# Sliding-window attention beside a Fourier mixing layer: transposed outputs written into the bytes of their chunk's sums, the halves in a tile of their own, and VectorE's sum of value products queued behind its latest low half

## The chip, the cores and the metric

The kernel runs on one core of a Trainium2 chip. The metric is the device time of one execution in microseconds (us). Three timed runs of the kernel before gave 1701.39, 1704.11 and 1705.67 us; the median is 1704.11 us. All engines named here belong to the one core: TensorE (PE in the profile; PEld is its weight load), VectorE (DVE), ScalarE (ACT), GpSimd (POOL) and SyncE (SP), which here issues nearly all DMAs.

## The reference

Two independent layers on a sequence of 2048 rows and 1024 columns; their outputs stand side by side. The first is attention with 32 heads of 32 columns, in which a query sees the 256 keys up to its own. The second multiplies by two Fourier matrices along the columns and two along the rows and keeps the real part.

```python
qkv = (x @ wqkv).reshape(B, S, 3, H, Dh)           # H = 32, Dh = 32
scores = einsum("bhqd,bhkd->bhqk", q, k) * Dh ** -0.5
mask = (i - j >= 0) & (i - j < 256)
o = einsum("bhqk,bhkd->bhqd", softmax(where(mask, scores, -1e9)), v)
a = o.reshape(B, S, D) @ wo

p = einsum("bsd,ed->bse", x, dft_hid_re); r = einsum("bsd,ed->bse", x, dft_hid_im)
b = einsum("ts,bse->bte", dft_seq_re, p) - einsum("ts,bse->bte", dft_seq_im, r)
out = concatenate([a, b], axis=-1)
```

## The kernel before

Every float32 operand is split into a high and a low half in float16, and a product is made of three float16 products (high by high, high by low, low by high). The big products are made first for the queries, keys and values, then for the Fourier layer in 48 units, then for the output projection. The units and the projection use a scheme of seven products for eight (the function `seven`, whose bank names a, b, c give the matmul names p_a, p_b, p_c).

Attention is not a stage of its own. It is a generator (`attention`) that the big products pull forward a step at a time (`tick`), from the value projection on to the last quarter of the Fourier layer. TensorE therefore runs one fixed stream in which attention's small matmuls stand between big ones: all matmuls that go through `mm` are held in program order.

Attention works on 256 blocks, each of 128 queries for two heads. Four blocks make a chunk; there are 64 chunks, and the names end in group, head pair and chunk, so that o_6_1_0 is chunk 52 counted from 0. For a block b:

- `s_step(b)`: TensorE writes the scores s (three PSUM banks in turn) and those of the farthest key block, far. VectorE masks them with a predicated copy (L259) and takes the maximum mx (L261). ScalarE makes the bias (L264), two exponentials (L271) and the high half hl (L274). VectorE makes the low half (L275). SP transposes both halves into t (L277).
- `z_step(b)`, two to four blocks later: GpSimd masks the transposed probabilities into z and t (L289, L291).
- `v_step(b)`, six blocks later and for two blocks at once (a pair; pair p is blocks 2p and 2p + 1, and its bank is named pv_2p): TensorE writes the value products, for the high and the low value columns, into the one PSUM bank with the tag "pv". VectorE adds the two (L323, a TENSOR_REDUCE) into the chunk's tile o. This sum frees the bank. The scale transposes of the Fourier units (pt_u) use the same bank.
- `o_step`, after a chunk's second sum: VectorE takes the reciprocal of the softmax sums (L332), GpSimd multiplies (L334), ScalarE and GpSimd split the product into the halves tile ohl (L337, L338), and SP transposes it into the tile ot (L340). The store of ot to the DRAM tensor ots (L360) waits in a list; it is issued in the step in which a fourth block of a chunk is started, behind the newest transpose.

The tiles o, ohl and ot of all chunks share one tag with three buffers: each new tile takes one that has been given back.

Each engine takes its instructions strictly in the order of its own queue. Where nothing in the code fixes the order, the compiler's scheduler sets it. `tc.issue_after(x)` tells the scheduler to place an instruction behind x in the queue; it adds no wait of its own. The list `behind` holds VectorE's latest low half: that of a block (L275), of a projection's output (L962, or L122 through `vec`), or the add that ends a Fourier product (L1045).

Of the kernel before, what the change touches and what calls it, by code (L numbers as in the profile page):

```python
# [9 lines left out]
F32 = mybir.dt.float32  # L10
F32R = mybir.dt.float32r
F16 = mybir.dt.float16
# [4 lines left out]
ALU = mybir.AluOpType  # L17
AX = mybir.AxisListType

P = 128  # L20
# [3 lines left out]
DH = 32  # L24
# [6 lines left out]
QB = CH // P  # L31
# [22 lines left out]
def fused_kernel(ctx: ExitStack, tc: tile.TileContext, xa, wqk, wv, wo, xb, wd, cs, out):  # L54
    nc = tc.nc
# [57 lines left out]
    def mm(*args, **kwargs):  # L113
        with tc.issue_after(fixed[0].ins) if fixed else nullcontext():
            fixed[:] = [nc.tensor.matmul(*args, **kwargs)]  # L115
        return fixed[0]
# [22 lines left out]
    behind = []  # L139
# [71 lines left out]
    def attention():  # L211
        att = cell["att"]
# [3 lines left out]
        st, cur, q2s, k2s, vts, store_o = {}, {}, {}, {}, {}, []  # L216
# [78 lines left out]
        def v_step(b):  # L295

            g, hp, sc, i = blocks[b]
            pvb = ps_v.tile([P, CH], F32, tag="pv", name=f"pv_{b}")
            pvt = pvb[:, :4 * VW].rearrange("p (r h w) -> p r h w", r=2, h=2)
            if (g, hp, sc) not in cur:  # L300
                cur[g, hp, sc] = att.tile([P, QB, 2, DH + 1], F32, tag="o", bufs=3, name=f"o_{g}_{hp}_{sc}")
            for r in (1, 0):
                qb = sc * QB + i + r
                nb = min(qb + 1, 3)
                nt = min(nb, 2)
                d = st[b + r]

                def weights(part, j, kb):
                    if nb == 3 and kb == 0:
                        return d["z"][:, part * 2 + j]  # L310
                    return d["t"][:, (part * 2 + j) * nt + kb - (nb - nt)]

                seq = [(0, kb) for kb in range(nb)] + [(1, kb) for kb in range(nb)]
                for j in range(2):
                    at = j * VW
                    for m, (part, kb) in enumerate(seq):
                        w = VW if part == 0 else DH + 1
                        k = qb + 1 - nb + kb
                        mm(pvt[:, r, j, :w], weights(part, j, kb),
                           vts[g, hp, k // QB][:, k % QB, at:at + w],  # L320
                                         start=(m == 0), stop=(m == len(seq) - 1),
                                         skip_group_check=True)
            nc.vector.tensor_reduce(cur[g, hp, sc][:, i:i + 2], pvt.rearrange("p r h (k w) -> p r h w k", k=2),  # L323
                                    axis=AX.X, op=ALU.add)
            del st[b], st[b + 1]

        def o_step(g, hp, sc):

            o = cur.pop((g, hp, sc))
            rs = att.tile([P, 2 * QB], F32, tag="rs", name=f"rs_{g}_{hp}_{sc}")  # L330
            on = o.rearrange("p i h w -> p (i h) w")
            nc.vector.reciprocal(rs, on[:, :, DH])  # L332
            on = on[:, :, :DH]
            nc.gpsimd.tensor_tensor(on, on, rs.unsqueeze(2).to_broadcast([P, 2 * QB, DH]), op=ALU.mult)  # L334
            o = o[:, :, :, :DH]
            ohl = att.tile([P, QB, 2, DH, 2], F16, tag="o", bufs=3, name=f"ohl_{g}_{hp}_{sc}")
            nc.scalar.activation(ohl[:, :, :, :, 0], o, AF.Copy)  # L337
            nc.gpsimd.tensor_tensor(ohl[:, :, :, :, 1], o, ohl[:, :, :, :, 0], op=ALU.subtract)  # L338
            ot = att.tile([P, QB, P], F16, tag="o", bufs=3, name=f"ot_{g}_{hp}_{sc}")
            nc.sync.dma_start_transpose(ot, ohl.rearrange("p i h d a -> p (i h d a)"))  # L340
            store_o.append((ots[sc, g, hp].rearrange("c a t -> (c a) t"), ot.rearrange("p i q -> p (i q)")))

        for b in range(nblk + LAG):
            for j in range(2):
                yield (blocks[b][0], blocks[b][2]) if b < nblk else None
                if b < nblk and j == 0:
                    s_step(b, 0)
                    s_step(b, 1)
                if j == 1 and b % 2 == 0 and b >= LAG:
                    v_step(b - LAG)  # L350
                    g, hp, sc, i = blocks[b - LAG + 1]
                    if i == QB - 1:
                        o_step(g, hp, sc)
                if j == 1 and b % 2 == ZAT and 3 <= b < nblk + 4:
                    for m in (b - 3 - (ZAT == 0), b - 2 - (ZAT == 0)):
                        if 0 <= m < nblk:
                            z_step(m)
                if j == 1 and store_o and (b >= nblk or blocks[b][3] == 3):
                    with tc.issue_after(line[0].ins):
                        nc.sync.dma_start(*store_o.pop(0))  # L360
                if j == 1 and b < nblk and blocks[b][3] == 1 and b + 3 < nblk:
                    g, hp, sc, _ = blocks[b + 3]
                    if (g, sc) in ready:
                        do_load(g, hp, sc)
                if j == 1 and b < nblk and blocks[b][3] == 3 and b + 1 < nblk:
                    g, hp, sc, _ = blocks[b + 1]
                    if (g, sc) in ready:
                        do_load_v(g, hp, sc)
# [526 lines left out]
    with tc.tile_pool(name="pa", bufs=3) as pa:  # L895
# [43 lines left out]
        for n, (kd, g, c) in enumerate(order):  # L939
# [12 lines left out]
            if kd == "v":  # L952
# [6 lines left out]
                f = vf[:, g, t // 4:t // 4 + 1]  # L959
# [137 lines left out]
    with tc.tile_pool(name="pb", bufs=1) as pb:  # L1097
# [45 lines left out]
        for n, (kind, p, c, i) in enumerate(units):  # L1143
# [35 lines left out]
            f = fu.pop(n)  # L1179
# [75 lines left out]
```

## Time and profile before

| what | before |
|---|---|
| median of 3 runs | 1704.11 us (1701.39 to 1705.67) |
| the profiled execution | 1701.5 us, of which the span is 1699.8 us |
| TensorE busy | 1688.6 us (99%) |
| VectorE busy | 1299.0 us (76%) |
| ScalarE busy | 1168.5 us (69%) |
| GpSimd busy | 575.2 us (34%) |
| sums of value products (L323) | 128, 425 ns each |
| stores of transposed outputs (L360) | 64, 128 KB each |

The profile is one execution. A row of the timeline gives the start and the length in us, the engine, the line, the operation, the tiles out<-in, and in square brackets how long the engine sat idle before it and what ended that. Buffer numbers are left out of the names there. A row of the waits gives who waited for whom, the total in us, how often, and the longest. Rows of one engine can overlap by about 0.1 us.

### The profile page before, as it was taken

The numbers are of one execution on the slowest core, as the hardware profiler recorded it, in microseconds if no ns is written. First come the engines' busy times: TensorE is split into PE (matmuls) and PEld (weight loads), VectorE is DVE, ScalarE is ACT, GpSimd is POOL, SyncE is SP. The second block draws the span as 40 slices with busy tenths as digits, with TensorE's granted clock in tenths as the row PEclk, the third lists the DMA queues.
The fourth block names the chain that finished last, engine by engine and source line by source line (L and its number), as shares of the span: only waits on it lengthen the run. The fifth ranks groups of instructions, "written<-read, shape, count | busy, mean of one in ns | idle before, by whom it ended". The sixth has DMA issues, their size and how long they took to land.

```text
span 1699.8 us, 30887 instructions
## 1 busy us (share of the span) xinstructions
PE 1688.6 (99%) x11007; PEld 847.7 (50%) x11007; DVE 1299.0 (76%) x2223; ACT 1168.5 (69%) x2035; POOL 575.2 (34%) x874
## 2 busy tenths in 40 slices
PE   9999999999999999999999999999999999999999
PEld 4444544555555555555554555545545545444444
DVE  7657787888987789897688896688876698687442
ACT  4476666676876787887787886688877688563322
POOL 0001222344434441444423565434555425411000
PEclk9999999999999999999999999999999999999999
DMA  6677999999999985987997999986989976866431
GB/s 244 240 267 245 252 289 269 282 264 306 256 240 209 211 220 127 206 194 184 232 251 236 199 186 176 227 197 127 190 161 204 226 183 137 177 180 121 115 99 75
DMA packets 469899, 348.63 MB, mean 205 GB/s; under 512 B 376944, under 2 KB 409968, under 8 KB 468848
## 3 DMA queue, kind: packets, MB, share of 16 engines
q1 hardware_dynamic: 462064, 321.48, 75.7%
q0 software_dynamic: 7680, 25.17, 9.5%
q8 instruction: 86, 1.41, 0.4%
q14 instruction: 69, 0.57, 0.1%
HBM read 166.99 MB, written 106.17 MB: 161 GB/s over the span
## 4 chain that ended last, share of the span: by engine, by line
PE 90%; DVE 3%; DMA 3%; ACT 2%; issue 1%; SPq 0%; POOL 0%; DVEq 0%; ACTq 0%; POOLq 0%
PE p_a L115 25%; PE pv L115 13%; PE p_b L115 12%; PE pq L115 10%; PE pk L115 10%; PE p_c L115 6%; PE po_a L115 5%; PE s L115 3%; PE po_b L115 2%; PE far L115 1%; PE po_c L115 1%; DMA ots<-ot 1%; DMA raw_wo<-in_wo_dram 1%; DVE reg L850 0%; DMA t<-hl 0%
## 5 line engine op out<-in xcount | busy, mean ns | idle before, releaser
L271 ACT ACTIVATE s<-s,bias,escs 128x256 f32<-128x256 f32 (+1 forms) x512 | 270.0, 528 | 11.7
L289 POOL TENSOR_SCALAR_AFFINE_SELECT z<-t 128x512 f16<-128x512 f16 x224 | 183.8, 828 | 162.2 <-PE pv L115 140.3
L264 ACT ACTIVATE bias<-mx,pshift,escs 128x2 f32<-128x2 f32 x256 | 98.4, 384 | 172.0 <-DVE mx L261 171.3
L275 DVE TENSOR_TENSOR hl<-s,hl 128x512 f16<-128x512 f32 (+1 forms) x256 | 170.2, 665 | 51.6 <-ACT hl L274 50.8
L115 PEld LDWEIGHTS <-reg 128*128 128x128 f16 x1344 | 128.9, 98 | 141.5
L291 POOL TENSOR_SCALAR_AFFINE_SELECT t<-t 128x512 f16<-128x512 f16 x224 | 187.8, 847 | 11.3
L115 PE MATMUL p_a<-reg,un_c 128*128 128x512 f16 x768 | 181.4, 379 | 0.6 <-DVE reg L850 0.3
L115 PE MATMUL pk<-reg,wu_k 128*128 128x512 f16 x768 | 174.2, 379 | 0.0
L268 POOL TENSOR_SCALAR mark<-bias 128x1 f32<-128x1 f32 x128 | 52.5, 410 | 358.3 <-ACT bias L264 333.6
L261 DVE TENSOR_REDUCE mx<-s 128x2 f32<-128x512 f32 (+1 forms) x256 | 170.9, 668 | 3.5
L115 PE MATMUL pv<-reg,reg 128*128 128x512 f16 x768 | 172.5, 379 | 0.0
L115 PEld LDWEIGHTS <-un_c 128*128 128x128 f16 x1152 | 109.9, 97 | 121.5 <-issue 2.2
L115 PEld LDWEIGHTS <-un_b 128*128 128x128 f16 x1152 | 109.6, 97 | 117.7 <-issue 0.9
L115 PEld LDWEIGHTS <-un_a 128*128 128x128 f16 x1152 | 109.4, 97 | 116.5
L115 PE MATMUL pq<-reg,wu_q 128*128 128x512 f16 x696 | 156.3, 379 | 0.0
L274 ACT ACTIVATE hl<-s 128x512 f16<-128x512 f32 (+1 forms) x256 | 148.8, 581 | 6.9 <-DMA t<-hl 1.4
L115 PE MATMUL p_a<-reg,un_b 128*128 128x512 f16 x576 | 136.4, 379 | 0.3 <-DVE y L1045 0.2
L115 PE MATMUL p_c<-reg,un_a 128*128 128x512 f16 x576 | 136.5, 379 | 0.0
L115 PE MATMUL p_b<-reg,un_b 128*128 128x512 f16 x576 | 136.3, 379 | 0.1
L115 PE MATMUL p_a<-reg,un_a 128*128 128x512 f16 x576 | 136.1, 379 | 0.0
L259 DVE COPY_PREDICATED s<-upper,far 128x256 f32<-128x256 uint32 x224 | 94.3, 421 | 46.3 <-PE s L115 45.3
L115 PEld LDWEIGHTS <-qk 96*128 96x128 f16 x1056 | 87.7, 97 | 66.4 <-issue 4.9
(216 smaller groups left out, 3139.7 us busy)
## 6 DMA issues: line engine op xcount, KB each, us to landing
raw_u<-in_cs_dram SPq DMA_DIRECT2D x64, 512.0 KB, 5.0
qk<-qk SPq DMA_DIRECT2D x64, 384.0 KB, 4.7
out_dram<-y POOLq DMA_DIRECT2D x72, 256.0 KB, 6.3
raw_wd<-in_wd_dram SPq DMA_DIRECT2D x24, 512.0 KB, 5.6
vs<-yv SPq DMA_DIRECT2D x32, 264.0 KB, 4.5
vt<-vs SPq DMA_DIRECT2D x64, 132.0 KB, 4.7
qk<-yq SPq DMA_DIRECT2D x32, 256.0 KB, 4.5
raw_wo<-in_wo_dram SPq DMA_DIRECT2D x16, 512.0 KB, 8.4
```

The source lines that it names most:

```text
L115: fixed[:] = [nc.tensor.matmul(*args, **kwargs)]
L259: nc.vector.copy_predicated(s[:, :, P:], upper2, d["far"] if nb == 3 else never2)
L261: nc.vector.tensor_reduce(mx, sv, axis=AX.X, op=ALU.max, negate=True)
L264: nc.scalar.activation(bias, mx, AF.Identity, bias=pshift, scale=es)
L268: marks[:] = [nc.gpsimd.tensor_scalar(mark, bias[:, 0:1], 1.0, None, op0=ALU.mult)]
L271: nc.scalar.activation(sv[:, h], sv[:, h], AF.Exp, bias=bias[:, h:h + 1], scale=es)
L274: nc.scalar.activation(hi, sv, AF.Copy)
L275: behind[:] = [nc.vector.tensor_tensor(lo, sv, hi, op=ALU.subtract)]
L289: nc.gpsimd.affine_select(out=z, in_=pk, compare_op=ALU.is_gt, fill=0.0, base=0, pattern=[[0, 4], [-1, P]], channel_multiplier=1)
L291: nc.gpsimd.affine_select(out=pk, in_=pk, compare_op=ALU.is_ge, fill=0.0, base=0, pattern=[[0, 4], [1, P]], channel_multiplier=-1)
```

## The change

Three things are edited.

- The chunk's tile o gets the tag to itself, with two buffers. The halves tile ohl gets a tag of its own with one buffer.
- The transposed output ot is no longer a tile. It is written, as float16, over the first 1024 of the 1056 bytes per partition of its own chunk's tile o, whose sums have been read by then. The store reads from there.
- The sum of value products is placed with `tc.issue_after(behind[0].ins)`, behind VectorE's latest low half.

Instructions, their shapes and the bytes moved stay the same. In the changed file the lines after the first edit stand one to three lower: the sum is L325, the reciprocal L335, the transpose L343, the store L363.

```diff
             if (g, hp, sc) not in cur:
-                cur[g, hp, sc] = att.tile([P, QB, 2, DH + 1], F32, tag="o", bufs=3, name=f"o_{g}_{hp}_{sc}")
+                cur[g, hp, sc] = att.tile([P, QB * 2 * (DH + 1)], F32, tag="o", bufs=2, name=f"o_{g}_{hp}_{sc}")
...
-            nc.vector.tensor_reduce(cur[g, hp, sc][:, i:i + 2], pvt.rearrange("p r h (k w) -> p r h w k", k=2),
-                                    axis=AX.X, op=ALU.add)
+            o = cur[g, hp, sc].rearrange("p (i h w) -> p i h w", i=QB, h=2)
+            with tc.issue_after(behind[0].ins):
+                nc.vector.tensor_reduce(o[:, i:i + 2], pvt.rearrange("p r h (k w) -> p r h w k", k=2),
+                                        axis=AX.X, op=ALU.add)
             del st[b], st[b + 1]
 
         def o_step(g, hp, sc):
 
-            o = cur.pop((g, hp, sc))
+            held_o = cur.pop((g, hp, sc))
+            o = held_o.rearrange("p (i h w) -> p i h w", i=QB, h=2)
...
-            ohl = att.tile([P, QB, 2, DH, 2], F16, tag="o", bufs=3, name=f"ohl_{g}_{hp}_{sc}")
+            ohl = att.tile([P, QB, 2, DH, 2], F16, tag="ohl", bufs=1, name=f"ohl_{g}_{hp}_{sc}")
...
-            ot = att.tile([P, QB, P], F16, tag="o", bufs=3, name=f"ot_{g}_{hp}_{sc}")
+            ot = held_o.bitcast(F16)[:, :QB * P].rearrange("p (i q) -> p i q", i=QB)
             nc.sync.dma_start_transpose(ot, ohl.rearrange("p i h d a -> p (i h d a)"))
             store_o.append((ots[sc, g, hp].rearrange("c a t -> (c a) t"), ot.rearrange("p i q -> p (i q)")))
```

TensorE's order is the same but for the scale transposes pt, of which some stand a few matmuls later. VectorE's order changes as follows at three places. In the rows, a name ends in the tile's number; a bracket names the semaphores that the instruction waits for, where DMAHW is a DMA queue and _49 only marks the build.

The first place is chunk 52's first sum (pair 104, blocks 208 and 209), in VectorE's queue of the kernel before.

```order
L261 TENSOR_REDUCE mx_214_15657<-s_214_15651 128x2 [waits DVE_49]
L122 SCALAR_TENSOR_TENSOR un33_a_15677<-raw_u33_0_15324,sc_u33_15635,un33_a_15677 128x1024 [waits DMAHW5_49,Activation_49]
L323 TENSOR_REDUCE o_6_1_0_15688<-pv_208_15687 128x132 [waits DMAHW3_49,DMAHW2_49,DMAHW6_49,DMAHW0_49,PE_49]
L807 TENSOR_TENSOR raw_u33_0_15324<-raw_u33_0_15324,raw_u33_1_15129 128x512 [waits DVE_49]
L275 TENSOR_TENSOR hl_213_15612<-s_213_15598,hl_213_15612 128x512 [waits DMAHW5_49,Activation_49]
L807 TENSOR_TENSOR raw_u33_1_15129<-raw_u33_1_15129 128x512 [waits DVE_49]
L259 COPY_PREDICATED s_215_15716<-upper_90,far_1040 128x2x128 [waits PE_49]
L261 TENSOR_REDUCE mx_215_15722<-s_215_15716 128x2 [waits DVE_49]
L122 SCALAR_TENSOR_TENSOR reg1_83<-raw_u33_1_15129,sc_u33_15635,reg1_83 128x512 [waits Activation_49]
L275 TENSOR_TENSOR hl_214_15663<-s_214_15651,hl_214_15663 128x512 [waits DMAHW2_49,Activation_49]
```

The same place in the changed kernel.

```order
L275 TENSOR_TENSOR hl_213_15560<-s_213_15546,hl_213_15560 128x512 [waits DMAHW5_49,Activation_49]
L122 SCALAR_TENSOR_TENSOR un33_a_15625<-raw_u33_0_15273,sc_u33_15583,un33_a_15625 128x1024 [waits DMAHW7_49,Activation_49]
L259 COPY_PREDICATED s_215_15664<-upper_90,far_1040 128x2x128 [waits PE_49]
L810 TENSOR_TENSOR raw_u33_0_15273<-raw_u33_0_15273,raw_u33_1_15079 128x512 [waits DVE_49]
L122 SCALAR_TENSOR_TENSOR reg1_83<-raw_u33_1_15079,sc_u33_15583,reg1_83 128x512 [waits Activation_49]
L261 TENSOR_REDUCE mx_215_15670<-s_215_15664 128x2 [waits DVE_49]
L275 TENSOR_TENSOR hl_214_15611<-s_214_15599,hl_214_15611 128x512 [waits DMAHW7_49,Activation_49]
L325 TENSOR_REDUCE o_6_1_0_15636<-pv_208_15635 128x132 [waits DMAHW4_49,DMAHW0_49,Pool_49]
L810 TENSOR_TENSOR raw_u33_1_15079<-raw_u33_1_15079 128x512 [waits DVE_49]
L259 COPY_PREDICATED s_216_15717<-upper_90,far_1040 128x2x128 [waits PE_49]
```

The sum stood ahead of the low halves of blocks 213 and 214 and of the masking of s_215; now it stands behind all three. It waits for DMA queues in both. Of the 64 first sums of a chunk, 10 wait for a DMA queue in the kernel before and 62 in the changed one.

The second place is chunk 54's second sum (pair 109, blocks 218 and 219), in VectorE's queue of the kernel before.

```order
L261 TENSOR_REDUCE mx_224_16285<-s_224_16281 128x2
L122 RECIPROCAL sc_u35_16254<-sc_u35_16254 128x1
L787 TENSOR_SCALAR fu35_16260<-fa_108,sc_u35_16254 128x1
L323 TENSOR_REDUCE o_6_1_2_16189<-pv_218_16309 128x132
L332 RECIPROCAL rs_6_1_2_16335<-o_6_1_2_16189 128x8
L122 SCALAR_TENSOR_TENSOR un35_a_16297<-raw_u35_0_15891,sc_u35_16254,un35_a_16297 128x1024
L259 COPY_PREDICATED s_225_16362<-upper_90,never_93 128x2x128
L807 TENSOR_TENSOR raw_u35_0_15891<-raw_u35_0_15891,raw_u35_1_15740 128x512
L122 SCALAR_TENSOR_TENSOR reg1_83<-raw_u35_1_15740,sc_u35_16254,reg1_83 128x512
L261 TENSOR_REDUCE mx_225_16366<-s_225_16362 128x2
L807 TENSOR_TENSOR raw_u35_1_15740<-raw_u35_1_15740 128x512
L275 TENSOR_TENSOR hl_224_16291<-s_224_16281,hl_224_16291 128x256
```

The same place in the changed kernel.

```order
L275 TENSOR_TENSOR hl_223_16190<-s_223_16176,hl_223_16190 128x512
L790 TENSOR_SCALAR fu35_16206<-fa_108,sc_u35_16200 128x1
L122 SCALAR_TENSOR_TENSOR un35_a_16243<-raw_u35_0_15838,sc_u35_16200,un35_a_16243 128x1024
L810 TENSOR_TENSOR raw_u35_0_15838<-raw_u35_0_15838,raw_u35_1_15688 128x512
L259 COPY_PREDICATED s_225_16307<-upper_90,never_93 128x2x128
L122 SCALAR_TENSOR_TENSOR reg1_83<-raw_u35_1_15688,sc_u35_16200,reg1_83 128x512
L810 TENSOR_TENSOR raw_u35_1_15688<-raw_u35_1_15688 128x512
L275 TENSOR_TENSOR hl_224_16237<-s_224_16227,hl_224_16237 128x256
L325 TENSOR_REDUCE o_6_1_2_16135<-pv_218_16255 128x132
L261 TENSOR_REDUCE mx_225_16311<-s_225_16307 128x2
L810 TENSOR_TENSOR raw_u35_1_15688<-raw_u35_1_15688,raw_u35_0_15838 128x512
L335 RECIPROCAL rs_6_1_2_16281<-o_6_1_2_16135 128x8
```

The sum moved behind the low half of block 224 and the five instructions in front of that; the reciprocal moved with it.

The third place is chunk 63's first sum (pair 126, blocks 252 and 253), near attention's end, in VectorE's queue of the kernel before.

```order
L122 RECIPROCAL sc_u44_18585<-sc_u44_18585 128x1 [waits DVE_49]
L787 TENSOR_SCALAR fu44_18591<-fa_108,sc_u44_18585 128x1
L122 SCALAR_TENSOR_TENSOR un44_a_18643<-raw_u44_0_18309,sc_u44_18585,un44_a_18643 128x1024 [waits DMAHW2_49,Activation_49]
L323 TENSOR_REDUCE o_7_1_3_18610<-pv_252_18609 128x132 [waits PE_49,Pool_49]
L807 TENSOR_TENSOR raw_u44_0_18309<-raw_u44_0_18309,raw_u44_1_18127 128x512 [waits DMAHW3_49,DVE_49]
L807 TENSOR_TENSOR raw_u44_1_18127<-raw_u44_1_18127 128x512 [waits DVE_49]
```

The same place in the changed kernel.

```order
L122 RECIPROCAL sc_u44_18522<-sc_u44_18522 128x1 [waits DVE_49]
L790 TENSOR_SCALAR fu44_18528<-fa_108,sc_u44_18522 128x1
L325 TENSOR_REDUCE o_7_1_3_18547<-pv_252_18546 128x132 [waits DMAHW5_49,DMAHW7_49,PE_49,Pool_49]
L122 SCALAR_TENSOR_TENSOR un44_a_18580<-raw_u44_0_18247,sc_u44_18522,un44_a_18580 128x1024 [waits DMAHW2_49,Activation_49]
L810 TENSOR_TENSOR raw_u44_0_18247<-raw_u44_0_18247,raw_u44_1_18066 128x512 [waits DMAHW3_49,DVE_49]
L810 TENSOR_TENSOR raw_u44_1_18066<-raw_u44_1_18066 128x512 [waits DVE_49]
```

Here the sum moved ahead, in front of the low half un44_a of a Fourier unit, and it waits for two DMA queues where it waited for none.

## The prediction

> **What bounds the kernel now.** I read the page's busy times first, then TensorE's busy time by stretches of 50 us, the waits, and last the timeline around the largest hole.
>
> ```profile
> span 1699.8 us, 30887 instructions
> PE 1688.6 (99%) x11007; PEld 847.7 (50%) x11007; DVE 1299.0 (76%) x2223; ACT 1168.5 (69%) x2035; POOL 575.2 (34%) x874
> ```
>
> TensorE is busy for all but 11.2 us of the span. Its matmul stream is the same after the change, so only holes can be won. The stretches with holes (start:end, length, TensorE busy, count, clock, DMA share, GB/s):
>
> ```profile
> 0.00:50.00 50.00, 48.42 (x168) 1.00 0.70 257
> 250.00:300.00 50.00, 48.88 (x326) 1.00 0.96 272
> 850.00:900.00 50.00, 49.72 (x323) 1.00 0.97 276
> 900.00:950.00 50.00, 49.67 (x345) 1.00 0.89 201
> 1200.00:1250.00 50.00, 46.57 (x338) 1.00 0.92 173
> 1650.00:1700.00 50.00, 45.85 (x225) 1.00 0.16 64
> ```
>
> The first (1.6 us) and the last (4.15 us, behind the last matmul) lie outside attention. Inside it there are 1.1, 0.3, 0.3 and 3.4 us; with 0.3 us in smaller ones that is 5.4 us, the most that any change of attention's waits can win in this execution. The waits, in order TensorE, VectorE, and SP's queue:
>
> ```profile
> PE far L115 <- DVE s L259: 4.3, 2, 3.2
> PE p_a L115 <- ACT p_c L1077: 0.2, 1, 0.2
> DVE o L323 <- PE pv L115: 27.0, 28, 2.2
> DVE o L323 <- DMA ots<-ot: 5.7, 1, 5.7
> SPq L340 <- DMA ots<-ot: 42.0, 26, 5.7
> ```
>
> TensorE's 4.3 us are two waits for VectorE's masking copy. The larger one follows from VectorE's 5.7 us for a store, as the rows of the three engines show:
>
> ```profile
> 1227.53 9.63 DMA ots<-ot
> 1230.39 1.29 DVE L122 SCALAR_TENSOR_TENSOR un_a<-raw_u,sc_u,un_a 128x1024 f16<-128x1024 f32 x1 [0.84 <-ACT un_a L128]
> 1232.85 0.22 PE L115 MATMUL far<-qk 96*128 96x128 f16 x1
> 1235.77 1.03 PE L115 MATMUL p_c<-reg,un_a 128*128 128x512 f16 x4
> 1237.38 0.43 DVE L323 TENSOR_REDUCE o<-pv 128x132 f32<-128x264 f32 x1 [5.70 <-DMA ots<-ot]
> 1239.53 0.42 DVE L259 COPY_PREDICATED s<-upper,far 128x256 f32<-128x256 uint32 x1
> 1240.01 0.22 PE L115 MATMUL far<-qk,qk 96*128 96x128 f16 x1 [3.21 <-DVE s L259]
> ```
>
> The store of chunk 50 is issued at 1227.53 and takes 9.63 us. Chunk 52's first sum has been given the buffer of that transposed output. VectorE reaches it at 1231.7 and stands until 1237.38, with the low half of block 213 and the copy of s_215 queued behind it. The copy comes at 1239.53, and TensorE, which needs the bank at 1236.8 (1240.01 less 3.21), loses 3.21 us.
>
> **The change part by part.** Instructions and bytes are the same, so only order and waits count. The sum is made against the profiled execution: 1701.5 us, the span of 1699.8 and 1.7 around it. The median of the runs, 1704.11, is 2.6 us above that; the other executions had more holes than this one.
>
> *The stall at chunk 52: −3.2 us.* In the new order the low half of block 213 and the copy of s_215 stand ahead of the sum. TensorE writes that block's scores at 1232.85, so the copy can run by about 1234.2, 2.6 us before TensorE asks. The sum itself still comes when the store has landed or shortly after, but behind it stand only the copy for block 216 and Fourier work. Bounds: 0 (something else is late at the same spot) to 3.2; I take all of it, because the row names the copy and nothing else is queued in front.
>
> *The 1.1 us wait near 294 us* follows a longer chain over GpSimd and ScalarE, in which the sum has no row; I leave it, bounds −1.1 to 0. So also the two holes of 0.3 us.
>
> *The transpose of SP.* It waited 42.0 us in 26 places for the store of the chunk before, since both used one buffer. Now it writes over its own chunk's sums and waits only for GpSimd's low half, which it needed before. SP is not on TensorE's path except through the transposed probabilities, and for those TensorE has no wait in the list. Worth 0, with some cover won.
>
> *The store's wait is now everywhere.* With two buffers, the sum of chunk n + 2 always overwrites bytes that the store of chunk n reads: 62 first sums wait for a store instead of 10. The stores' landing, over all 64:
>
> ```profile
> L360 SPq DMA_DIRECT2D ots<-ot x64: 319/570/2020, 202.8 to 1476.9; - x64
> DMA to landing us min/median/max: 1.9/3.6/9.6
> ```
>
> Issue to landing takes 3.6 us in the median. The step that issues a store is three blocks ahead of the sum that needs it. The moved sums stand one to two low halves later in VectorE's queue, which raises the cover. The exception is attention's end, where blocks no longer follow: there the new order puts chunk 63's sum in front of un44_a, and it now waits for the store of chunk 61.
>
> ```profile
> 1458.97 0.57 SPq L360 DMA_DIRECT2D ots<-ot  x1
> DMA to landing us min/median/max: 6.3/6.3/6.3
> 1462.50 0.43 DVE L323 TENSOR_REDUCE o<-pv 128x132 f32<-128x264 f32 x1
> 1469.96 0.43 DVE L323 TENSOR_REDUCE o<-pv 128x132 f32<-128x264 f32 x1 [1.14 <-PE pv L115]
> 1461.30:1469.90 8.60, 5.41 (x9) 1.00 0.86 176
> ```
>
> The last row is VectorE's busy time from the start of un44_a to the last sum: 5.41 us of work in 8.60. The store lands at 1458.97 + 6.3 = 1465.3. In the new order all of that work stands behind the sum that waits for it, so the last sum starts at 1465.3 + 5.4 = 1470.7 instead of 1469.96, 0.8 us late. Behind it hang reciprocal, halves, transpose, store, and then the loads of wo, which wait for attention's memory:
>
> ```profile
> 1486.74 9.34 DMA raw_wo<-in_wo_dram
> 1495.98 0.69 ACT L1043 ACTIVATE y<-p_a,fu 128x512 f32<-128x512 f32 x1 [4.09 <-PE p_a L115]
> 1496.57 1.14 ACT L128 ACTIVATE reg<-raw_wo,sc_wo 128x1024 f16<-128x1024 f32 x1
> ```
>
> The load landed at 1496.08, 0.5 us before ScalarE was free for it; and TensorE waited 0.2 us for the p_c copy of the same queue. So 0.8 us late costs 0.8 − 0.5 = 0.3 us or a little more: +0.5, bounds 0 and +4 (a store that takes 9.6 as at chunk 50). [...]
>
> *The bank is given back later: +0.5 us.* There is one value bank, and the next pair's matmuls or a scale transpose need it. For each of the 128 sums I took from the timeline the end of the instruction that the new order puts in front, added the sum's own 0.34 us, took off what the sum no longer costs ahead of it, and compared with TensorE's next use in the new order. 98 sums move back; the median cover is 3.8 us. A usual pair (58) and the tightest kind (109), each with the old sum, the low half that now goes first, and TensorE's next use:
>
> ```profile
> 760.73 0.42 DVE L323 TENSOR_REDUCE o<-pv 128x132 f32<-128x264 f32 x1
> 762.38 0.68 DVE L275 TENSOR_TENSOR hl<-s,hl 128x512 f16<-128x512 f32 x1
> 767.03 0.19 PE L115 MATMUL pv<-vt,z 128*128 128x66 f16 x1
> ...
> 1280.43 0.42 DVE L323 TENSOR_REDUCE o<-pv 128x132 f32<-128x264 f32 x1
> 1286.06 0.41 DVE L275 TENSOR_TENSOR hl<-s,hl 128x256 f16<-128x256 f32 x1
> 1286.53 0.19 PE L115 MATMUL pv<-vt,z 128*128 128x66 f16 x1
> ```
>
> At pair 58 the bank would be free at 763.4, 3.6 us early. At pair 109 it would be free at 1286.8, or 1286.4 without the sum's old place ahead of the half, with TensorE there at 1286.53: cover 0.1. Seven pairs have under 1 us, 12 under 1.5, 22 under 2. By this execution's times nothing is lost (−0.1 in all). Over all pairs, low halves that come 0.5 us later would cost 1.4 us, 1.0 us 4.0, 1.5 us 8.4. They should rather come earlier, since VectorE no longer stands 27.0 us in front of them for TensorE. I take +0.5.
>
> Sum: 1701.5 − 3.2 + 0.5 + 0.5 = 1699.3. Of the other executions' 2.6 us I keep half, since a store's wait is as much by chance as their surplus: 1700.6 us.
>
> **The rivals.**
>
> *The late bank decides.* Place: TensorE's pv and pt matmuls. For it: VectorE 76% busy with queued Fourier work ahead of many low halves, one bank, twelve covers under 1.5 us. Against: the VectorE stalls that go. From 1.0 us of lateness the gain is gone; at 1.5 us the time is 1701.5 − 3.2 + 0.5 + 8.4 + 1.3 = 1708.5, slower than before. [...]
>
> *The stall only changes place.* 62 sums wait for stores; one of 9.6 us at a chunk with a cover under 4 us stops VectorE again, for the 3.2 us at TensorE that we saw, and the change wins nothing: 1701.5 + 0.5 + 0.5 + 1.3 = 1703.8. For it: chunks 10, 20 and 41, whose first sums are not moved. Against: in this execution the covers hold.
>
> *All holes close.* The waits near 294 and 900 us come from VectorE's order too, and the other executions' surplus is store stalls: 1701.5 − 3.2 − 1.1 − 0.6 + 0.5 = 1697.1.
>
> **How the numbers follow.** Forecast (1699 to 1703) 0.5, all holes close 0.2, the stall changes place 0.15, the late bank 0.15. About 0.3% (5.1 us) is what a measurement of this kernel can tell from no change: faster is below 1699.0, slower above 1709.2. Faster: 0.2 and 0.07 of the forecast's low edge, 0.27. Slower: two thirds of the late bank, 0.1. The same: 0.63. The range runs from 1696.8 (all holes closed) to 1707.0, short of the late bank's 1708.5; the forecast's own is 1699 to 1703.
>
> **What would show it.** Right: no row of VectorE's sums waiting over 2 us for a store before 1400 us; the wait of SP's output transpose for a store gone; VectorE's wait for TensorE's value products far below 27.0 us; the stretch 1200 to 1250 at 49.5 us of TensorE or more. The tail term: chunk 63's sum waiting 4 to 6 us for a store. Wrong: a row of TensorE's pv or pt matmuls waiting for VectorE's sum, with several us in total; TensorE's busy time itself changed; or holes where no moved instruction stands.

## The result and the profile after

The changed kernel takes 1717.8 us (median of 6 runs, 1714.9 to 1726.5) against 1703.8 us for the kernel before (median of 6 runs beside it, 1701.2 to 1707.1). The ratio is 1.0092, with a 95% interval of 1.0068 to 1.0116: slower by 14 us, where 1700.6 us was forecast. In the experiments below, one slow execution of 6716.8 us, of the run with the tiles alone, is left out. The execution that was profiled is one of the longer ones: 1726.5 us, of which 1724.7 are the span.

The first lines of the page after:

```profile
span 1724.7 us, 31043 instructions
PE 1694.9 (98%) x11007; PEld 848.2 (49%) x11007; DVE 1302.6 (76%) x2223; ACT 1166.8 (68%) x2035; POOL 571.5 (33%) x874
```

TensorE runs the same number of matmuls but is busy 6.3 us longer, and its idle time has grown from 11.2 to 29.8 us. TensorE's stretches of 50 us (start:end, length, busy, count, granted clock, DMA share, GB/s):

```profile
250.00:300.00 50.00, 50.00 (x332) 1.00 0.97 276
900.00:950.00 50.00, 43.92 (x279) 0.93 0.72 205
1000.00:1050.00 50.00, 47.57 (x327) 1.00 0.93 156
1200.00:1250.00 50.00, 49.62 (x372) 1.00 1.03 189
1250.00:1300.00 50.00, 48.19 (x361) 1.00 1.02 177
1450.00:1500.00 50.00, 43.99 (x311) 0.93 0.82 135
```

The two largest holes that the kernel before had inside attention are closed (250 to 300, and 1200 to 1250 where 46.57 had been). Two deep ones are new, at 900 and 1450, each with a lower clock, and there are shallow ones from 1000 to 1300. The waits after, TensorE first, then VectorE's sums:

```profile
PE pv L115 <- DVE o L325: 6.0, 1, 6.0
PE p_b L115 <- ACT un_b L128: 3.4, 1, 3.4
PE pv L115 <- DVE sc_u L122: 2.9, 5, 0.8
PE p_b L115 <- DVE un_b L122: 2.7, 1, 2.7
PE p_a L115 <- DVE y L1048: 1.8, 3, 0.8
PE far L115 <- DVE s L259: 1.2, 4, 0.3
DVE o L325 <- DMA ots<-o: 13.7, 1, 13.7
DVE o L325 <- PE pv L115: 2.2, 3, 1.4
```

By single matmuls, and without one of 1.2 us at the very start that every run has, TensorE has 25 holes of more than 0.15 us where it had 7: three of 2 us and more (3.4 and 2.7 near 905, 6.0 at 1492) and 22 smaller ones of 12.4 us in all, against 2.4 us of such small ones before.

**The hole near 905 us.** TensorE waits for the second low half (un_b) of Fourier unit 16. From the timeline of the kernel before, the scale transpose of that unit, what VectorE makes of it, and TensorE's use of un_b:

```profile
882.61 0.22 PE L176 MATMUL pt_u<-unit,top_u 128*128 128x128 bf16 x1
883.20 0.28 DVE L122 TENSOR_REDUCE sc_u<-pt_u 128x1 f32<-128x128 f32 x1
894.45 1.28 DVE L122 SCALAR_TENSOR_TENSOR un_b<-raw_u,sc_u,un_b 128x1024 f16<-128x1024 f32 x1
898.76 2.99 PE L115 MATMUL p_b<-reg,un_b 128*128 128x512 f16 x12
```

The same after, with the sum that frees the bank first:

```profile
888.08 0.42 DVE L325 TENSOR_REDUCE o<-pv 128x132 f32<-128x264 f32 x1
890.50 0.22 PE L176 MATMUL pt_u<-unit,top_u 128*128 128x128 bf16 x1
891.03 0.28 DVE L122 TENSOR_REDUCE sc_u<-pt_u 128x1 f32<-128x128 f32 x1
906.83 1.27 DVE L122 SCALAR_TENSOR_TENSOR un_b<-raw_u,sc_u,un_b 128x1024 f16<-128x1024 f32 x1
904.84 0.61 PE L115 MATMUL p_b<-reg,un_b 128*128 128x512 f16 x2 [3.37 <-ACT un_b L128]
908.15 2.31 PE L115 MATMUL p_b<-reg,un_b 128*128 128x512 f16 x5 [2.70 <-DVE un_b L122]
```

Up to here the matmul stream runs 2.5 us later than before, but the transpose comes 7.9 us later and un_b 12.4 us later. In the orders, the transpose of unit 16 has fallen 24 matmuls back. It is one of 17 scale transposes that did, by 2 to 24 matmuls and 203 in all. They are not made through `mm`, so nothing holds them in the fixed stream; they use the value bank, and the scheduler places each where the bank has been given back.

The moved transposes cost at the bank too. At all five places where TensorE waits for sc_u (2.9 us in the waits above, none before), a value product stands right behind a transpose that fell back by 16 to 22 matmuls, and waits until VectorE has read the bank.

### The profile page after: what moved, and what is told of

Same layout as the page of the kernel before. It is cut to its first block, busy times and chain, and to the rows that moved or that the text cites. A ratio compares the mean times of both kernels' runs of the same rounds, so it can differ in the third digit from the quotient of the medians.

```text
span 1724.7 us, 31043 instructions
## 1 busy us (share of the span) xinstructions
PE 1694.9 (98%) x11007; PEld 848.2 (49%) x11007; DVE 1302.6 (76%) x2223; ACT 1166.8 (68%) x2035; POOL 571.5 (33%) x874
## 4 chain that ended last, share of the span: by engine, by line
PE 80%; DVE 7%; ACT 6%; issue 3%; DMA 3%; POOL 1%; SPq 0%; DVEq 0%; POOLq 0%; ACTq 0%
PE p_a L115 20%; PE pv L115 13%; PE p_b L115 10%; PE pk L115 10%; PE pq L115 9%; PE p_c L115 5%; PE po_a L115 5%; PE s L115 3%; PE po_b L115 2%; PE far L115 1%; PE po_c L115 1%; DMA ots<-o 1%; DVE hl L275 1%; ACT s L271 1%; DVE raw_u L810 1%
## 5 line engine op out<-in xcount | busy, mean ns | idle before, releaser
L291 POOL TENSOR_SCALAR_AFFINE_SELECT t<-t 128x512 f16<-128x512 f16 x224 | 195.0, 885 | 9.7
```

Of the source, the lines that this page charges most:

```text
L291: nc.gpsimd.affine_select(out=pk, in_=pk, compare_op=ALU.is_ge, fill=0.0, base=0, pattern=[[0, 4], [1, P]], channel_multiplier=-1)
```

## The experiments

Three theories stood at first. A: the moved sums hand the bank over later, the scale transposes fall back, and the units' halves come late. B: with two buffers, first sums wait for stores. C: each moved sum costs a little by itself; in the first texts because the bank comes free later and value products wait, in the later ones through VectorE's order. In the texts on record a pair is called by its first block, as in the bank's name pv_144, so "pair 144" there is blocks 144 and 145. "Moved" means queued behind the latest low half. All ratios are to the kernel before.

### The two parts apart

```diff
 # tiles alone: the change without
-            with tc.issue_after(behind[0].ins):
 # order alone: the kernel before with
+            with tc.issue_after(behind[0].ins):
```

> Edit: the tiles of the change alone (transposed output in the bytes of its chunk's sums, two such buffers, halves in a tile of their own); VectorE's sums keep their old places, and every engine's order is that of the kernel before. Theory A (the moved sums hand the value bank over later, and the scale transposes that take it fall back in TensorE's stream): nothing of that is left here, 1702 to 1705 us, no difference from before (1703.8). Theory B (two buffers: 62 first sums wait for a store instead of 10, and some stores land late): most of the loss is here, 1710 to 1718 us, with rows of VectorE's sums waiting for stores of 5 us and more. Theory C (every moved sum frees the one bank later, and TensorE's value products wait): as A, 1702 to 1705.

> Edit: the order alone (the sum behind the latest low half); the tiles are those of the kernel before, three buffers shared by sums, halves and transposed outputs. The orders of all engines are those of the whole change. Theory A: the loss is here, 1713 to 1718 us, and the stall of about 6 us near 905 us, where VectorE's halves of un16 come late, is in the trace. Theory B: 1702 to 1706, without that stall. Theory C: 1713 to 1718, but spread over small waits of TensorE for sums.

Tiles alone: 1718.4 us (median of four), 1.0092 (1.0077 to 1.0107). Order alone: 1725.1 us, 1.0126 (1.0113 to 1.0139), above every theory's range. Each part costs as much as both together or more. So A or C holds for the order and B for the tiles, and they cover each other in part. The waits of the tiles alone show two places, chunk 52's first sum and chunk 63's:

```profile
PE far L115 <- DVE s L259: 11.4, 3, 9.5
PE pv L115 <- DVE o L324: 5.4, 1, 5.4
DVE o L324 <- DMA ots<-o: 23.0, 2, 11.6
```

The 9.5 us are the old stall of 3.2 us at chunk 52, grown: the store of chunk 50 takes 14.3 us there. In the whole change this sum is moved, and the stall is gone. The order alone has the hole near 905 and 29 small holes of 15.0 us.

### Sixteen sums

```diff
+        BEFORE_SCALE = {98, 102, 108, 112, 118, 144, 150, 154, 168, 190, 198, 202, 206, 210, 216, 250}
-            with tc.issue_after(behind[0].ins):
+            with nullcontext() if b in BEFORE_SCALE else tc.issue_after(behind[0].ins):   # all but the 16
+            with tc.issue_after(behind[0].ins) if b in BEFORE_SCALE else nullcontext():   # only the 16
```

> Edit: the whole change, but 16 of the 128 sums keep their old order: those that hand the value bank to a unit's scale transpose that the change had moved back. Of the 203 matmuls by which transposes had moved back, 24 are left, 17 of them at u18. Theory A: the loss is gone but for a wait or two, 1702 to 1707 us, no stall near 905 us. Theory B: as the whole change, 1715 to 1718. Theory C: 112 of 128 sums are still moved, so seven eighths of the loss of 14 us stays, 1714 to 1717.

> Edit: the mirror of it: the tiles of the change, and of the sums only these 16 are queued behind the latest low half; the transposes lie 198 matmuls later in all, as in the whole change. Theory A: nearly the whole loss, 1712 to 1717 us, with the stall near 905 us. Theory B: as the tiles alone, 1710 to 1718, and the same as that run within 2 us. Theory C: one eighth of the loss, 1704 to 1707.

All but the 16: 1711.8 us, 1.0073 (1.0047 to 1.0100), without the hole near 905. Only the 16: 1719.8 us, 1.0100 (1.0086 to 1.0115), with that hole, with 4.5 us for chunk 63's sum, and with 3.4 us left at chunk 52. No theory's range holds the first: A is right for the deep hole, but the 112 other sums cost too, 23 holes and 11.4 us. The second is within 2 us of the tiles alone, as B said. With shared bytes in both, stores blur the rest, so the next runs have the tiles of before.

### One sum, and two sums

```diff
 # the kernel before
-            nc.vector.tensor_reduce(cur[g, hp, sc][:, i:i + 2], ...
+            with tc.issue_after(behind[0].ins) if b in (144,) else nullcontext():    # (18, 208) in the other
+                nc.vector.tensor_reduce(cur[g, hp, sc][:, i:i + 2], ...
```

> Edit: the kernel before, with a single sum of the 128 queued behind the latest low half: that of pair 144 (the first of chunk 36), which hands the value bank to the scale transpose of unit 16. In TensorE's order only that transpose moves, 24 matmuls back. Theory A (the late bank acts through the scale transposes): VectorE's halves of un16 come late and TensorE stands some 6 us near 900 us, with the lost clock behind it 8 us in all: 1710 to 1713. Theory C (the loss is spread over all moved sums): 1703 to 1704, no difference.

> Edit: the kernel before, with two sums queued behind the latest low half: that of pair 18, which stands ahead of the wait of 1.1 us near 294 us, and that of pair 208, the first of chunk 52, which stood for the store of chunk 50. No scale transpose moves. By the step on the stall at chunk 52, 3.2 us go, and 1.1 to 1.3 near 294 us: 1698.5 to 1700.5. If something else is late at the same spots: 1702 to 1704.

One sum moved: 1708.9 us, 1.0042 (1.0028 to 1.0057). A single 0.4 us instruction, moved back in VectorE's queue, costs 5.9 us by the medians, 7.8 us of TensorE's delay at that place in the profile. Part of it comes back at chunk 52, where TensorE waits 1.8 us for the masking copy instead of 3.2. That is a little less than expected, and no stretch but this one is slower:

```profile
888.03 0.22 PE L176 MATMUL pt_u<-unit,top_u 128*128 128x128 bf16 x1
902.37 0.65 PE L115 MATMUL p_b<-reg,un_b 128*128 128x512 f16 x2 [3.37 <-ACT un_b L128]
905.68 4.26 PE L115 MATMUL p_b<-reg,un_b 128*128 128x512 f16 x10 [2.66 <-DVE un_b L122]
```

Two sums moved: 1697.6 us (1697.0 to 1698.3 in 11 runs), 0.9968 (0.9955 to 0.9980). It beats both kernels. The first lines of its page, with TensorE as busy as before:

```profile
span 1695.8 us, 30890 instructions
PE 1688.6 (100%) x11007; PEld 847.7 (50%) x11007; DVE 1298.4 (77%) x2223; ACT 1168.6 (69%) x2035; POOL 579.2 (34%) x874
```

Its stretches near 294 us and of chunk 52, both full (columns as above):

```profile
250.00:300.00 50.00, 50.00 (x332) 1.00 0.99 271
1200.00:1250.00 50.00, 49.68 (x377) 1.00 1.01 194
```

### The other 112 sums

In the change's profile, VectorE's low halves of units are stretched at a few places. One of them, with GpSimd's masks beside it, and the matmul that waits next (the ScalarE copy it waits for had itself stood behind 4.15 us of waiting for VectorE's maximum):

```profile
1010.11 3.59 DVE L122 SCALAR_TENSOR_TENSOR un_b<-raw_u,sc_u,un_b 128x1024 f16<-128x1024 f32 x1
1009.94 1.50 POOL L289 TENSOR_SCALAR_AFFINE_SELECT z<-t 128x512 f16<-128x512 f16 x2
1011.12 1.50 POOL L291 TENSOR_SCALAR_AFFINE_SELECT t<-t 128x512 f16<-128x512 f16 x2
1017.87 1.89 PE L115 MATMUL p_b<-reg,un_b 128*128 128x512 f16 x8 [0.83 <-ACT y L1046]
```

In the kernel before, the same un_b took 1.28 us (at 997.25). Theory D: the moved sums shift GpSimd's masks, and where four of them run back to back, VectorE's low half, which reads two SBUF tensors, stands until they are through. To try it, the masks of the ten blocks concerned were left out, first with the shared bytes, then with the tiles of before.

```diff
+            if b in (162, 163, 166, 167, 170, 171, 174, 175, 218, 219):
+                d["z"] = pk
+                return
```

> Edit: the change with the 16 sums in their old order (1711.8 us), and GpSimd's two causal masks left out for ten blocks (162, 163, 166, 167, 170, 171, 174, 175, 218, 219), those whose masks ran beside a VectorE low half of a unit that took 2.2 to 5.0 us instead of 1.3; the outputs of these blocks are not the reference's. No other instruction moves on VectorE or TensorE. Theory D (moving sums shifts GpSimd's masks onto VectorE's low halves, which read two SBUF tensors; VectorE is held up and TensorE waits behind it): those halves are back at 1.3 us and TensorE's holes from 981 to 1030 and near 1284 us shrink: 1706 to 1709. Theory C (VectorE's changed order alone): 1711 to 1713.

> Edit: the tiles of the kernel before, and 112 sums queued behind the latest low half; the 16 that hand the bank to a moved scale transpose keep their old order. The stores' waits of the shared bytes are out of it. From the holes of the earlier run with the same sums (11 us in small holes, 4.7 us won near 294 us and at chunk 52): 1708 to 1711 in all executions, with VectorE's low halves of units at 2.2 to 5.0 us near 980, 1000, 1020, 1041 and 1277 us. If the small holes belong to the shared bytes: 1697 to 1700.

> Edit: the run before, and GpSimd's two causal masks left out for the ten blocks 162, 163, 166, 167, 170, 171, 174, 175, 218 and 219, whose outputs are then not the reference's. Theory D (GpSimd's masks hold up VectorE's low halves that read two SBUF tensors): 4 to 6 us faster than the run before, 1703 to 1706, those halves at 1.3 us. Theory C (VectorE's changed order alone): within 1 us of the run before.

With shared bytes: 1712.0 us, 1.0050 (1.0031 to 1.0069), the same median as with the masks, but over 18 us (1702.0 to 1720.2). By its median that is what C said and not D; over such a spread it decides nothing. With the tiles of before: 1708.6 us with the masks, 1.0038 (1.0024 to 1.0052), and 1705.4 us without, 1.0012 (1.0001 to 1.0022). The group of the 32 un_b by form (busy us, mean ns), in the two-sum kernel:

```profile
L122 DVE SCALAR_TENSOR_TENSOR un_b<-raw_u,sc_u,un_b 128x1024 f16<-128x1024 f32 x32 | 43.6, 1363 | 1.5 <-ACT un_b L128 1.4
```

The same group with 112 sums:

```profile
L122 DVE SCALAR_TENSOR_TENSOR un_b<-raw_u,sc_u,un_b 128x1024 f16<-128x1024 f32 x32 | 50.2, 1568 | 2.6 <-ACT un_b L128 2.5
```

And with 112 sums, without the masks of the ten blocks:

```profile
L122 DVE SCALAR_TENSOR_TENSOR un_b<-raw_u,sc_u,un_b 128x1024 f16<-128x1024 f32 x32 | 42.4, 1324 | 1.6 <-ACT un_b L128 1.5
```

So D is a part, 3.2 us where 4 to 6 were expected. That may be too little: without these masks, those of other blocks stand beside three un_a halves, which now take 2.2 to 2.9 us, and the largest hole of the run (1.5 us at 994) ends 3.4 us behind one of them. The rest of what these sums cost is 1705.4 against 1697.6 with two sums. This run has 14 small holes of 6.6 us where the two-sum kernel has 5 of 1.5 us, most of them for VectorE's adds and ScalarE's copies. C as first put is out: TensorE's value products wait 0.2 us for a sum.

The 112 sums still move a few scale transposes, u18's by 17 matmuls and u14's by 8; behind each of these two TensorE has no hole over 0.15 us for the next 60 us, so A has little part in the rest. That the rest comes from VectorE's changed order is what remains; no run takes it alone.

### The shared bytes

```diff
 # tiles of the change, two sums moved
+            with tc.issue_after(behind[0].ins) if b in (18, 208) else nullcontext():
 # and, in the last chunk, the sums in a buffer of the probabilities' halves
-                cur[g, hp, sc] = att.tile([P, QB * 2 * (DH + 1)], F32, tag="o", bufs=2, ...
+                cur[g, hp, sc] = att.tile([P, QB * 2 * (DH + 1)], F32, tag="hl" if last else "o", ...
```

> Edit: the tiles of the change, and only the sums of pairs 18 and 208 queued behind the latest low half; all orders are those of the kernel before with these two sums moved (1697.6). Theory B (two buffers cost what the first sums of chunks 52 and 63 wait for stores, and nothing elsewhere): the stall at chunk 52 goes, that at chunk 63 stays: 1719 less 9.5 at chunk 52, less 1.3 near 294 us, less 1.3 of lost clock, 1705 to 1708. If the tiles cost something in many places: 1710 and more.

> Edit: as the run before, and the sums of the last chunk (63) in one of the buffers of the halves of probabilities, which are free by then, so that its first sum waits for no store. Theory B: both stalls of the tiles are gone, 1696 to 1699, the same as the kernel before with the two sums alone. If the tiles cost something else: 1701 and more.

> Edit: none against the run with the last chunk's sums apart (1702.3 us); a second profile, since its first was of its fastest execution (1699.4). If the tiles' transposes make the traffic near 1460 us late: a hole of 2 to 8 us there where TensorE's value products wait for GpSimd's masks, and 1702 to 1707. If chance alone: no hole over 1 us behind 1300 us.

With chunk 52's sum moved: 1706.0 us, 1.0016 (0.9997 to 1.0034), 1697.5 to 1714.0. With the last chunk's sums apart as well: 1702.3 us, 1.0004 (0.9992 to 1.0015), and in the repeat 1706.1 us, 1.0025 (1.0006 to 1.0045). Over both that is a median of 1703.4 us of 19 runs, 1699.4 to 1713.1. The first fits B by its median, but not by its profile, in which TensorE also waits 3.5 us at 961, where B has nothing. The second does not fit: with no sum waiting for a store, and every engine's order that of the two-sum kernel, the shared bytes still cost some 5.8 us, and every execution differs. In the second profile the two largest holes, 3.1 us at 961 and 2.4 us at 1244 (the first profile has the latter too, 2.3 us), both follow a wait for a transpose of probabilities. At 961 GpSimd's mask waits for one that took 12.0 us (6.6 in the two-sum kernel), and behind the mask come ScalarE's un_b and VectorE's sc_u, for which TensorE waits. At 1244 ScalarE's high half waits for one, and TensorE for the copy behind it.

```profile
954.74 0.64 POOL L289 TENSOR_SCALAR_AFFINE_SELECT z<-t 128x512 f16<-128x512 f16 x1 [3.96 <-DMA t<-hl]
961.00 0.19 PE L115 MATMUL pv<-vt,z 128*128 128x66 f16 x1 [3.07 <-DVE sc_u L122]
...
1242.11 0.60 ACT L274 ACTIVATE hl<-s 128x512 f16<-128x512 f32 x1 [4.84 <-DMA t<-hl]
1244.21 1.02 PE L115 MATMUL p_a<-reg,un_c 128*128 128x512 f16 x4 [2.42 <-ACT y L1048]
```

In all, ScalarE's high halves wait 9.7 us for such transposes in this profile, and 1.6 us in the two-sum kernel's.

The whole change was treated in the same way:

> Edit: the whole change, and the sums of the last chunk (63) in one of the buffers of the halves of probabilities, so that its first sum waits for no store; no order changes. If the stall there (6.0 and 8.3 us in two profiles, with lost clock behind it) is what sets the changed kernel's executions near 1725 and above apart from those near 1717: 1714 to 1718 with none above 1720. If that stall is also in the faster executions: 1707 to 1712.

1723.4 us, 1.0122 (1.0102 to 1.0141), none below 1719.7: a miss. The hole at chunk 63 stays, with another name. In this run TensorE waits for GpSimd's mask, which waits for the transposed probabilities:

```profile
1473.06 2.37 SPq L277 DMA_TRANSPOSE t<-hl  x1
1475.52 0.54 SPq L365 DMA_DIRECT2D ots<-o  x1
1479.03 2.09 SPq L345 DMA_TRANSPOSE o<-ohl  x1
1492.78 0.64 POOL L289 TENSOR_SCALAR_AFFINE_SELECT z<-t 128x512 f16<-128x512 f16 x1 [13.78 <-DMA t<-hl]
1493.47 0.24 PE L115 MATMUL pv<-vt,z 128*128 128x66 f16 x1 [7.94 <-POOL z L289]
```

The transposes of the last blocks, four output writes, the store of chunk 61 and chunk 62's output transpose are in flight together and land between 1488.6 and 1493.3. The transpose in the first row lands 19.6 us after its issue here, 12.7 and 19.9 in the change's two profiles and 7.7 in the kernel before. Two waits end with that traffic, the sum's for the store and the mask's for the probabilities; curing one leaves the other.

Is the traffic late because SP no longer holds the output transpose until the store has landed? The store of chunk 61 took 6.1 to 12.8 us in six profiles with the tiles of before, where chunk 62's output transpose goes out after it has landed, and 8.4 to 17.5 us in ten with shared bytes, where it goes out beside it. That leans to yes, but overlaps. Chunk 50's store speaks against it as the whole cause: there the next chunk's output transpose goes out beside the store with either tiles, and in the order with two sums moved it still takes 9.6 us with those of before and 11.6 to 11.8 us in three profiles with shared bytes. To hold the transpose again, a small read of the earlier store's bytes was put ahead of it:

```diff
+            if n >= 0:
+                nc.sync.dma_start(held_o.bitcast(F16)[0:1, :32], ots[n % NCH, n // (2 * NCH), n // NCH % 2, 0, 0:1, :32])
             nc.sync.dma_start_transpose(ot, ohl.rearrange("p i h d a -> p (i h d a)"))
```

> Edit: the tiles of the change with pairs 18 and 208 moved and the last chunk's sums apart (1702.3 us, 1699.4 to 1707.4), and ahead of each output transpose a read of 64 bytes of what the store of the chunk before wrote, into the bytes that the transpose overwrites: the transpose waits again until that store has landed, as in the kernel before, plus the landing of the read. If it is the transposes beside the stores in flight that make loads and transposes late: 1697 to 1700, and within 3 us of each other as for the kernel before with the two sums moved (1697.0 to 1698.3). If not, or if the reads themselves hold SyncE's queue: 1702 and more.

1729.9 us, 1.0150 (1.0120 to 1.0180). The reads hold SP's queue themselves:

```profile
SPq L348 <- DMA o<-ots: 121.3, 56, 7.7
SPq L347 <- DMA ots<-o: 62.5, 31, 8.7
```

So this says nothing on the question. Another try gave the transposed output a place in the rotation of GpSimd's masks z:

```diff
-            ot = held_o.bitcast(F16)[:, :QB * P].rearrange("p (i q) -> p i q", i=QB)
+            ot = att.tile([P, QB, P], F16, tag="z", bufs=3, name=f"ot_{g}_{hp}_{sc}")
```

> Edit: old order of the sums; two buffers for sums alone, one for halves, and the transposed output in the rotation of the three buffers that hold GpSimd's z, so that no sum waits for a store. Theory B (what the tiles cost is the sums' wait for a store): the stalls near 1247 and 1480 us of the tiles alone are gone, and so is the 3.2 us of the kernel before: 1699 to 1702. If the cost of the tiles is the transposes that run beside the stores (late transposed probabilities, late loads): 1710 to 1718 still.

1753.0 us, 1.0297 (1.0277 to 1.0318). No sum waits for a store, but TensorE waits 27.1 and 16.9 us for GpSimd's two masks, in 31 places: z's buffers became the bound. It cannot speak on B. Why the shared bytes make this traffic late stays open.

### The changed kernel once more

> Edit: none, the changed kernel once more, for a second profile. Theory A: the stall near 905 us is there again, at 8 us with the lost clock. Theory B: if the stall of 6 us for the store of chunk 61 near 1490 us is chance, it is missing where the time is near 1717, and there where it is near 1725.

One execution of 1732.0 us. The hole near 905 is there to 0.01 us (3.4 and 2.7 us); the one at chunk 63 is 8.3 us, for a sum that stood 16.0 us. Up to 1384 us this execution runs 17.5 us behind the kernel before, and the first one 16.9. So in these two the body agrees to 0.6 us, and the tail differs by chance. 1726.5 less the 8.0 us of delay in the tail would be 1718.5, where the shorter executions are; none of those was profiled.

## Why the prediction was wrong

It forecast 1700.6 us and no change; the kernel is 14 us slower. The moved order alone costs 21.8 us and the tiles alone 15.1, where the prediction had −2.7 and +0.5. By its steps:

- **"Its matmul stream is the same after the change, so only holes can be won."** This premise failed. The part on the change even notes that some scale transposes stand a few matmuls later in TensorE's order, and the prediction gave that no price. A transpose that falls 24 matmuls back is not 24 matmuls of lost time; it is a link of a chain (top, transpose, scale, three halves on VectorE) that must end before a fixed point of the stream. The runs price it: one such sum costs 5.9 us, and order alone with all sums is 16.5 us slower than with the 112 (1725.1 less 1708.6). Only the one sum's path was taken alone; that all 16.5 us run over transposes is argued.
- **"The bank is given back later: +0.5 us."** It is the term that failed. It asked only whether TensorE's next use of the bank stands and waits. That is small, though not the +0.5: TensorE waits 1.0 us in a transpose for a sum, and 2.9 us in five value products behind moved transposes. What the later sum moves in the queues of VectorE and GpSimd was not in it. The 112 sums that move hardly any transpose bring 1708.6 us where the two useful ones alone bring 1697.6: the other 110 cost 11.0 us, 3.2 of it by GpSimd's masks of ten blocks. In sum, order alone is −5.5 for two sums, +11.0 and +16.5, or +22.0 (measured +21.8).
- **"The stall at chunk 52: −3.2 us."** Right to 0.2 us: the matmul there comes 3.4 us earlier, in the change and in the two-sum kernel.
- **"The 1.1 us wait near 294 us ... in which the sum has no row; I leave it."** Wrong, in the good direction: with the second sum of chunk 4 moved, 1.3 us go.
- **"The transpose of SP ... Worth 0."** The wait is gone as foreseen. But with both first-sum waits cured the shared bytes still cost 5.8 us, and this wait is the one thing of theirs that is then left out of SP's order. That it was keeping the traffic apart is argued, not shown, and at chunk 50 it can't be what makes the store late.
- **"The store's wait is now everywhere": +0.5, bounds 0 to +4.** The place was right, attention's end, and before 1400 us no sum waits 2 us for a store. The size was not: the sum stood 13.7 and 16.0 us instead of 4 to 6, since the store took 15.3 and 17.5 us where the bound had 9.6. Lost clock came on top (0.50 from 1490 to 1495). Without the moved order chunk 52 would have paid too (9.5 us).
- **The rivals.** "The late bank decides" (0.15) named the right resource and the right side, and that its 1708.5 us is nearly what the 112 sums give is luck. Its path, TensorE's pv and pt matmuls standing for the bank, cost 3.9 us of the change's 24.5 us in holes.
- **What would show it wrong** was well chosen: TensorE's busy time did change, and holes stand where no moved instruction stands.

## What to carry to other kernels

When an edit moves an instruction that frees a shared bank, list everything that takes that bank, and follow what it feeds to its deadline, not just to its next wait; an instruction that the scheduler may place freely falls back silently. Here an order rule was worth applying where a profile shows a wait and nowhere else: two sums of 128 gave 5.5 us, the other 126 took back 27.5. Before two tiles share bytes, ask whether a wait that looks idle has been keeping two transfers apart; here that stayed open.

## What the runs showed of the hardware

**A hole costs more than its idle time.** TensorE's stretches of 5 us in the change, around the two deep holes (the number behind the count is the granted clock):

```profile
900.00:905.00 5.00, 1.63 (x8) 1.00 1.03 429
905.00:910.00 5.00, 2.30 (x7) 0.57 1.00 401
910.00:915.00 5.00, 5.00 (x19) 0.75 0.76 273
...
1490.00:1495.00 5.00, 2.69 (x29) 0.50 0.18 49
```

Near 905 two holes of 6.0 us in all delayed the stream by 7.8 us in the one-sum kernel, with a clock of 0.50 from 903 to 908: ten matmuls of p_b, from 905.68 on, took 4.26 us, where all twelve took 2.99 us before. The 3.21 us hole of the kernel before kept its clock at 1.00; the 6.0 us hole of the change ends in the stretch with 0.50. The mean clock of the profiled executions is 1.000 for the kernel before and for the repeat of the cured tiles (holes of 3.1 and 2.4 us), and 0.996 for the change and for the tiles with two sums (4.8 and 3.5 us).

**A unit's low half and GpSimd's masks take longer beside each other.** A low half of 1.28 us took 3.6 us beside four masks of 0.9 us, and it ended 1.1 us after the last. With 112 sums and the tiles of before it took 3.59 us too, and 1.27 us with those masks left out. In the kernel before it took its 1.28 us at 997.25, and the mask that started beside it at 997.42 took 1.61 us, where the next two took 0.63 and 0.64 us. The low half of a block, which reads one tensor in SBUF and one in PSUM, took 0.68 us at 998.78 beside the first of these two.

**Landing times depend on company.** In the change's first profile a 128 KB store took 1.7 us with no other transfer in flight (chunk 62's) and 15.3 us beside transposes and output writes (chunk 61's).
